# Chunk 4's projections and chunk 1's output projection as row pairs, in other stages

## The chip, the cores and the metric

The kernel runs on one core of one Trainium2 chip. The metric is the device time of one launch in microseconds (us), the median of several runs. TensorE is called PE, VectorE DVE, ScalarE ACT, GpSimd POOL and SyncE SP, as in the profile.

## The reference

One block of a transformer over 2048 rows of 576 columns, in bf16. `c` gives six rows of modulation. Attention is local: each row looks at 8 rows, itself and every second row before it; there are 32 heads of 18 columns.

```python
mod = (_silu(c) @ w_mod).reshape(c.shape[0], 6, 1, -1)
sa, ca, ga, sb, cb, gb = ...
h = _layernorm(x) * (1 + ca) + sa
x = x + ga * _A_ref(h, A_wqkv, A_wo)         # local attention, W = 8, dil = 2
h = _layernorm(x) * (1 + cb) + sb
x = x + gb * _B_ref(h, B_w_gate, B_w_up, B_w_down)   # ((h @ w_gate) * (h @ w_up)) @ w_down
```

The wide layer has 4608 columns, so nearly all of PE's work is gate, up and down.

## The kernel before

**Tiles and stages.** The rows are 8 chunks of 256 (`CH`), each of 2 tiles of 128 rows (`ST`). Chunks go through the wide layer in the groups `[[0], [1, 2], [3, 4], [5, 6], [7]]` (`GROUPS`). A setup does chunk 0's attention and part of the next chunks'. Then each group has a *gate/up* stage (36 column tiles `f`, `gate_up`) and a *down* stage (36 row tiles `f`, `down`). Projections, attention and norms of later chunks are put between the matmuls of these stages. The first gate/up takes chunk 0 (256 columns for each matmul) and has beside it chunk 3's Q, K and V, chunk 1's attention, and the start of chunk 2's. The first down has, before the change, chunk 4's Q, K and V, chunk 1's output projection and second norm, and chunk 2's values and output projection.

**Two forms of matmul.** 576 is four and a half times 128. In the plain form (`a_q`, `a_v`, `b_w`) a product takes five matmuls of 128 rows, and the rows 64 to 127 of the fifth (`KF`) hold zeros. In the paired form (class `Pair`: gate/up, `qk_pair`, `v_pair`, `w_pair`) two products run at once in the upper and the lower 64 rows, nine steps each, and swap halves between `first` and `second`. Then the fifth row tile must hold the same 64 rows twice: `both_halves` and `wo_both` copy these rows in the weights (on POOL, L1325 and L871), and the norm writes the last 64 columns a second time (argument `both`, L298 and L307), so that the transposed tile has them in both halves. A pair's matmuls are queued so that the next pair's `first` goes ahead of this pair's `second`. A pair holds two of PSUM's eight banks (`psp`); they are freed when ACT has cast them (L821, L822: `u_sb`, `g_sb`) or DVE has read them.

**The order.** Every engine runs its instructions in the order of the program. `timed` plans it: `items` are the stage's own column tiles with their PE time, `extra` are the pairs to be put between them, and `threads` are lists of pieces `(PE time, DVE time, what it needs, its mark, wait until the mark holds, call)`. The planner counts a time `t` for PE and one for DVE, and issues a piece when its need is marked by then and DVE isn't too far behind. What is left when a gate/up stage ends (`late`) goes into the following down. `gbg` holds the lists of each gate/up, `first_down` and `next_down` those of the downs.

**Chunk 1's second norm.** `b_w(1, j)` multiplies `oT` by `wo` and DVE adds the result to the row (L659 to L663); `b_ln(1)` takes the statistics on DVE; `b_norm(1)` normalizes on ACT (L290 to L308); `b_td(1)` transposes with two DMAs from SP's queue into `h2T` (L689), and `b_mod(1)` modulates that tile, its column blocks 3 and 4 on ACT (L325), 0 to 2 on DVE (L323). The second gate/up begins with chunk 1's half of it. `b_o(2)` is the transpose of chunk 2's attention on PE, with two copies to `oT` on ACT (L577, L578); `b_w(2, j)` uses `oT`. `a_t4` transposes chunk 4's normalized rows on PE.

**DMA queues.** SP issues the gate/up weights (L158), rows (L140, L144) and transposes. POOL issues the down weights (`load_wd`, L175), the write of V to DRAM (`vd`) and its reading with the eight offsets (`b_ld`, L481, 1152 KB). `behind` makes a DMA wait for another's landing. Blocks of down weights that have no buffer of their own are put in memory that is free for a while: blocks 5 and 6 of the first group in `prod_t` (`ld_prods(0)`), once the products of chunk 2 have been used.

Of the kernel before, what the change touches and what calls it, by code (L numbers as in the profile page):

```python
# [22 lines left out]
KF = 4  # L23
# [16 lines left out]
GC = D // 4  # L40

GROUPS = [[0], [1, 2], [3, 4], [5, 6], [7]]
PAIRED = (3, 5, 7)


@with_exitstack
def kernel(
# [13 lines left out]
    nc = tc.nc  # L61
# [259 lines left out]
    def modulate(dst, s, m, vi_scale, vi_shift, on_dve):  # L321
        if on_dve:
            nc.vector.tensor_scalar(dst, s, modc[:, vi_scale, m:m + 1], modc[:, vi_shift, m:m + 1], ALU.mult, ALU.add)  # L323
        else:
            nc.scalar.activation(dst, s, ACTF.Identity, bias=modc[:, vi_shift, m:m + 1], scale=modc[:, vi_scale, m:m + 1])  # L325

    def transposed(src, dst, cols, vi):
        n = P * len(cols)
        pA = ps([P, 3, n], BF, "tr_pA")
        pB = ps([P, 2, n], BF, "tr_pB")  # L330
        for m in range(KT):
            d = pA[:, m, :] if m < 3 else pB[:, m - 3, :]
            for c, j in enumerate(cols):
                nc.tensor.transpose(d[:, js(c)], src[:, j, m * P:(m + 1) * P], ident[:])

        def evict(first_on_dve=True):
            for m in range(KT):
                s = pA[:, m, :] if m < 3 else pB[:, m - 3, :]
                modulate(dst(m), s, m, vi + 1, vi, (m < 3) == first_on_dve)
        return evict  # L340

    def mod_columns(wm, pi, fill=lambda: None, steps={}, order=(KF, 0, 1, 2, 3)):
# [49 lines left out]

    def a_ln(i):
        x = x_in.pop(i)
        xn, rsq, norm = layernorm(lambda j: x[:, j, :], "a", i in (3, 4), i in (3, 5, 6, 7))
        aa[i] = dict(xn=xn, rsq=rsq, norm=norm)

    def a_norm(i):
# [21 lines left out]
            nc.sync.dma_start_transpose(out=aa[i]["hT"][:, :, js(j)], in_=aa[i]["xn"][:, j, :])  # L420

    def a_t4():
        a_t(4, False)
        nc.gpsimd.memset(aa[4]["hT"][64:, KF, :], 0.0)

    def a_mod(i, ms, on_dve=True):
        hT = aa[i]["hT"]
# [47 lines left out]
    def b_ld(i, j):  # L475
        b = bb.setdefault(i, dict(prod={}, vsh={}))
        base = HALO + i * CH + j * P - DIL * (W - 1)
        vsh = vshp.tile([P, W, DH, H], BF, name="vsh")
        vsrc = bass.AP(vd.tensor, vd.offset + base * D, [[D, P], [DIL * D, W], [1, D]])
        b["vsh"][j] = vsh  # L480
        return nc.gpsimd.dma_start(vsh[:].rearrange("p w d h -> p w (d h)"), vsrc)  # L481

    def b_p(i, w):
        b = bb.setdefault(i, dict(prod={}, vsh={}))
# [240 lines left out]
    def values_of(i, nxt=None):  # L725
        r = []
        for j in range(ST):
            r += [(0, 0.75, f"a{i}", "-", 0, lambda j=j, w=w: b_mul(i, j, w)) for w in range(0, W, 2)]
            r += [(0, 0.75, "", "-", 0, lambda j=j: b_add(i, j, 0)), (0, 0.75, "", "-", 0, lambda j=j: b_add(i, j, 1)),
                  (0, 1.2, "", f"o{i}{j}", 0, lambda j=j: b_add(i, j, 2))]  # L730
            if i in PAIRED:
                r.append((0, 0, "", f"O{i}" if j == ST - 1 else "-", 11.0 if i == 7 else 14.0, lambda j=j: b_od(i, (j,))))
            if nxt is not None:

                r.append((0, 0, f"v{nxt}", "-", 0, lambda j=j: behind(b_ld(nxt, j), bb[i]["od"]) if (i, j) == (3, 1) else b_ld(nxt, j)))
        return r
# [153 lines left out]

    QKP = [(0, 1), (2, 3), (4,), (5, 6), (7, 8)]

    def timed(items, extra, threads, slack, busy=0.0):

        t, dve = 0.0, busy
        done, seq = {f"v{i}": 0.0 for g in GROUPS for i in g[1:]}, []
        done["late"] = 0.0
        extra, threads = list(extra), [list(th) for th in threads]

        def ready(need):  # L900
            return all(done.get(x, 1e9) <= t for x in need.split())

        def fill():
            nonlocal t, dve
            moved = True
            while moved:
                moved = False
                for th in threads:
                    if th and ready(th[0][2]) and (not th[0][1] or dve <= t + slack):
                        pe, d, _, mark, wait, call = th.pop(0)  # L910
                        t += pe
                        dve = max(dve, t) + d if d else dve
                        done[mark] = (dve if d else t) + wait
                        seq.append(("piece", call))
                        moved = True
                        break
        for kind, f, step, own, need in items:
            if seq and extra and ready(extra[0][1]):
                pe, _, mark, make, *ve = extra.pop(0)
                seq.append(("pair", make))  # L920
                t += pe
                dve = max(dve, t) + sum(ve)
                done[mark] = t + pe + 1.0
                fill()
            assert ready(need), (need, t)
            seq.append((kind, f))
            fill()
            dve = max(dve, t) + own
            t += step
        assert not extra, (extra[0][1], t)  # L930
        return seq, [(*p[0:2], p[2] if all(x in names(th) for x in p[2].split()) else "late", *p[3:]) for th in threads for p in th]

    def names(th):
        return [p[3] for p in th]
# [397 lines left out]
    def ld_prods(gi):  # L1332
        for k in range(2):
            g = gi * NBLK + (5 if gi == 0 else 3) + k
            wd_home[g] = prod_t[:, k * FB * D:(k + 1) * FB * D].rearrange("p (k d) -> p k d", d=D)
            r = load_wd(g)
            if gi:
                behind(r, wgu_in[gi * NBLK + NBLK - 1])

    loads = {(0, 23): lambda: behind(load_wd(1), bb[2]["ltd"]), (0, 24): lambda: ld_d1(4), (0, 25): lambda: load_wd(2), **{(gi, 32): lambda gi=gi: ld_prods(gi) for gi in (1, 2, 3)}, (3, 34): wgu_spaces, (NG - 1, 28): lambda: [ld_spare(k) for k in range(4)]}  # L1340

# [5 lines left out]
    def gb_row():  # L1347
        gb_cols(lambda k: wm5()[:, k, :] if k < KF else wm5r[:])
        ld_d1(3)

    first = attention_of(1, 2)[12:-14]
    first = [(0, 0, "", "p17", 2.2, nop), (0.75, 0, "p17", "l14", 1.0, lambda: b_l(1, 4)), (0.35, 0, "l14", "t14", 0.3, lambda: b_lt(1))] + first

    first[1:8] = [first[1], first[3], first[4], first[2], first[7], first[5], first[6]]
# [2 lines left out]
    at = [k for k, p in enumerate(first) if p[2] == "v2"][0]  # L1357
    first.insert(at + 4, (0, 0, "v2", "-", 0, lambda: behind(b_ld(2, 0), wgu_in[8])))
    first.pop(at)
    at = [k for k, p in enumerate(first) if p[3] == "o11"][0] + 2  # L1360
    first.insert(at, (0, 0, "o11", "O1", 0, nop))
    gbg = {0: (qkv_of(3, "p17 z3"),
               [[(0, 0, "", "-", 0, lambda: (load_wm5(), load_wd(0))), (0, 0, "", "z3", 8.0, both_halves), (0, 0, "", "w5", 12.0, nop), (0.85, 0, "w5", "-", 0, gb_row), (0, 0, "", "-", 0, lambda: load_res(2))],
                norm_of(3, "", "", 5) + [(0, 2.5, "", "m4", 0.2, lambda: a_ln(4)), (0, 0, "m4", "r4", 1.0, lambda: aa[4]["rsq"]()),
                                         (0, 0, "r4", "e4", 2.0, lambda: aa[4]["norm"]((0,))), (0, 0, "e4", "n4", 1.6, lambda: aa[4]["norm"]((1,))),
                                         (0, 0, "n4 v3", "x4", 0, nop)],
               first, [(0, 0, "y1", "s1", 0.6, lambda: b_exp(1))]]),
           1: (qkv_of(5, "p37") + wo_of(3),
               [[(0, 0, "", "-", 0, lambda: (loads_v(3), load_res(3), load_res(4), wo_both()))], norm_of(5, "p33", "", 7), second]),
           2: (qkv_of(6, "") + wo_of(5),  # L1370
               [[(0, 0, "", "h6", 1.0, lambda: (loads_v(5), load_res(5), load_res(6)))], attention_of(5, 6)]),
           3: (qkv_of(7, "") + wo_of(7), [[(0, 0, "", "h7", 1.0, lambda: load_res(7)), (0, 0, "v7", "-", 0, lambda: loads_v(7))], [(0, 0, "q74", "-", 0, nop)] + prods_of(7) + softmax_of(7) + values_of(7)]),
           4: ([], [])}

    def first_down(late):
        def q(g):
            return (0.53 if g == 2 else 1.07, 0, "h4", "-", 0, lambda: a_q(4, g))

        def v(j):
            return (1.2, 0, "h4", "-", 0, lambda: a_v(4, j))  # L1380

        def out_1(first):
            return [(0, 0, "", "o0", 0.4, nop), (0.55, 0, "o0", "o1", 1.9, lambda: b_o(1)), (1.2, 1.35, "o1", "-", 0, lambda: b_w(1, 0)), (1.2, 1.35, "", "x1", 0.5, lambda: b_w(1, 1)),
                    (0, 2.5, "", "s1", 0.7, lambda: b_ln(1)), (0, 0, "s1", "n1", 2.3, lambda: b_norm(1)), (0, 0, "n1", "t1", 9.5, lambda: b_td(1)),
                    (0, 1.0, "t1", "-", 0, lambda: (b_mod(1, (3, 4), False), b_mod(1, (0, 1, 2), True)))]
        assert not {"O1", "x4"} & set(names(late))
        a4 = [(0.6, 0, "", "h4", 1.7, lambda: (a_t4(), load_x(6), ld_prods(0)))]
        o2 = [(0, 0, "o21", "z2", 0.6, nop), (0.55, 0, "z2", "O2", 1.1, lambda: b_o(2)), (1.2, 1.35, "O2", "-", 0, lambda: b_w(2, 0)), (1.2, 1.35, "", "x2", 0.2, lambda: b_w(2, 1)),
              (0, 2.2, "", "s2", 0.7, lambda: b_ln(2)), (0, 1.5, "s2", "n2", 0.2, lambda: b_norm(2)), (0.55, 1.0, "n2", "-", 0, lambda: b_t(2))]
        return [a4, out_1(True), late + [(0, 0, "", "a2", 0.0, nop)] + values_of(2) + o2, [q(0), q(1), q(2), q(3), q(4), v(0), v(1)]]  # L1390

    def norm2_of(i, need):
        return [(0, 2.3, need, f"s{i}", 0.7, lambda: b_ln(i)), (0, 1.5, f"s{i}", f"n{i}", 0.2, lambda: b_norm(i)),
# [12 lines left out]
    left = []  # L1406
    for gi, grp in enumerate(GROUPS):
# [13 lines left out]
        if gi == NG - 1:  # L1421
            down_last(gi, hh)
        else:
            left = down(gi, hh, first_down(late) if gi == 0 else next_down(gi, late))
            assert gi == 0 or not left


# [28 lines left out]
```

## Time and profile before

| what | us |
|---|---|
| median of 3 runs | 540.21 (540.2 to 541.58) |
| the profiled execution | 540.27 |
| its span | 538.0 |
| first gate/up, in the trace | 48.1 to 94.0 |
| first down | 94.0 to 125.7 |
| second gate/up, begins | 125.7 |
| PE busy | 531.7 |
| DVE, ACT, POOL busy | 318.4, 253.0, 73.1 |

Windows of the trace over these stages give the share of the other engines: in the first gate/up (45.9 us) DVE is busy 37.1 us and ACT 35.4, in the first down (31.7 us) DVE 22.4 and ACT 14.1. Busy time of PE is from the start of a matmul to its modelled end, so that a matmul's duration (0.27 us for 256 columns) is longer than the step from one to the next; steps are read from the starts. A wait is the idle time of an engine in front of an instruction and is put down to what came last.

### The profile page before, as it was taken

To read this page: it belongs to the slowest core of one execution; us is meant where nothing else is said; L and a number is where in the kernel's file an instruction comes from. 1 tells how busy PE (TensorE), PEld (TensorE's weight loads), DVE (VectorE), ACT (ScalarE), POOL (GpSimd) and SP (SyncE) were. 2 spreads that over 40 slices of the span, in tenths; PEclk is the share of its full clock that TensorE was granted. 3 is DMA by queue.
4 is the path that set the end of the run, shared out by engine and by line. 5 is a ranking of instruction groups with operands and counts; after the bars stand their busy time and mean duration, and the time that the engine had idled before them with its cause. 6 is when DMAs were issued, how large, how long until landed. Compare 5 with 4: busy or idle time off the path is not lost.

```text
span 538.0 us, 14722 instructions
## 1 busy us (share of the span) xinstructions
PE 531.7 (99%) x6244; PEld 321.2 (60%) x6244; DVE 318.4 (59%) x731; ACT 253.0 (47%) x620; POOL 73.1 (14%) x113
## 2 busy tenths in 40 slices
PE   8999999999999999999999999999999999999997
PEld 4787888657745454555544454555544454558875
DVE  5899787858766788527467797514527733032212
ACT  4866877634656553013555543104556542006630
POOL 8105013212000110111000010110010101110210
PEclk9999999999999999999999999999999999999999
DMA  9999999889853862999345964973395694759731
GB/s 288 286 290 366 311 266 339 299 138 351 282 145 92 269 198 45 247 291 310 104 156 130 232 211 128 224 233 111 102 306 160 158 302 81 233 139 297 254 96 41
DMA packets 94659, 114.47 MB, mean 213 GB/s; under 512 B 27873, under 2 KB 83378, under 8 KB 94466
## 3 DMA queue, kind: packets, MB, share of 16 engines
q1 hardware_dynamic: 82864, 66.92, 45.5%
q0 software_dynamic: 11424, 46.40, 28.3%
q8 instruction: 49, 0.80, 0.7%
q10 hardware_dynamic: 306, 0.21, 0.1%
q14 instruction: 16, 0.13, 0.1%
HBM read 103.07 MB, written 4.74 MB: 200 GB/s over the span
## 4 chain that ended last, share of the span: by engine, by line
PE 96%; DVE 2%; DMA 1%; SPq 0%; issue 0%; ACT 0%
PE pg L770 28%; PE pu L770 23%; PE acc L1007 20%; PE pq L442 4%; PE pq L770 3%; PE accr L1012 3%; PE acc L1062 3%; PE pv L770 2%; PE pw L659 2%; PE pv L465 2%; PE lgT L499 1%; DMA wmA<-in_w_mod_dram 1%; PE pw L770 1%; PE po L614 1%; DVE prod_t L487 1%; PE pwj L636 0%
## 5 line engine op out<-in xcount | busy, mean ns | idle before, releaser
L770 PE MATMUL pg<-h2T,wgu 64*128 64x512 bf16 (+1 forms) x1376 | 266.4, 331 | 0.0
L770 PE MATMUL pu<-h2T,wgu 64*128 64x512 bf16 (+1 forms) x1376 | 265.5, 331 | 0.0
L770 PEld LDWEIGHTS <-wgu 64*128 64x128 bf16 x2752 | 133.9, 94 | 94.8
L821 ACT CAST u_sb<-pu 128x512 bf16<-128x512 f32 (+1 forms) x172 | 85.6, 498 | 150.5 <-PE pg L770 150.0
L824 DVE TENSOR_TENSOR hh<-g_sb,u_sb 128x512 bf16<-128x512 bf16 x136 | 58.3, 429 | 115.0 <-ACT g_sb L822 114.0
L822 ACT CAST g_sb<-pg 128x512 bf16<-128x512 f32 (+1 forms) x172 | 86.7, 504 | 0.0
L1007 PE MATMUL acc<-wd,hh 128*128 128x512 bf16 x344 | 86.1, 380 | 0.0
L1007 PEld LDWEIGHTS <-hh 128*128 128x128 bf16 x504 | 49.0, 98 | 59.2 <-issue 1.5
L1012 PE MATMUL accr<-wd,hh 128*128 128x64 bf16 x344 | 62.4, 193 | 0.0
L770 PE MATMUL pu<-h2T,wgr 64*128 64x512 bf16 (+1 forms) x188 | 61.4, 327 | 0.5 <-DVE dd L528 0.5
L770 PE MATMUL pg<-h2T,wgr 64*128 64x512 bf16 (+1 forms) x188 | 61.4, 327 | 0.0
L1012 PEld LDWEIGHTS <-hh 128*128 128x128 bf16 x504 | 45.8, 98 | 1.2
L175 POOL DMA_DIRECT2D wd<-in_B_w_down_dram x29 | 21.9, 754 | 173.7 <-PE accr L1012 138.1
L548 DVE TENSOR_TENSOR vsh<-vsh,attn 128x1152 bf16<-128x1152 bf16 x56 | 39.8, 752 | 0.0
L487 DVE TENSOR_TENSOR prod_t<-qT,kT 128x1280 bf16<-128x1280 bf16 x36 | 28.3, 820 | 3.3 <-ACT kT L841 2.7
L1007 PE MATMUL acc<-prod_t,hh 128*128 128x512 bf16 x112 | 28.2, 380 | 0.0
L770 PEld LDWEIGHTS <-wgr 64*128 64x128 bf16 x376 | 18.5, 94 | 15.8 <-issue 2.8
L481 POOL DMA_DIRECT2D vsh<-vd x14 | 12.6, 899 | 95.7 <-DVE o_sb L556 76.1
L325 ACT ACTIVATE h2T<-h2T,modc 128x256 bf16<-128x256 bf16 x12 | 6.6, 593 | 33.6 <-DMA h2T<-xn 33.6
L442 PE MATMUL pq<-hT,wqk 128*128 128x256 bf16 (+1 forms) x225 | 21.7, 251 | 0.1
L770 PE MATMUL pq<-hT,wqk 64*128 64x256 bf16 (+1 forms) x360 | 21.6, 258 | 0.0
L1012 PE MATMUL accr<-prod_t,hh 128*128 128x64 bf16 x112 | 21.6, 193 | 0.0
(225 smaller groups left out, 627.7 us busy)
## 6 DMA issues: line engine op xcount, KB each, us to landing
wgu<-in_B_w_gate_dram SPq DMA_DIRECT2D x41, 512.0 KB, 5.0
wgu<-in_B_w_up_dram SPq DMA_DIRECT2D x41, 512.0 KB, 6.8
wd<-in_B_w_down_dram POOLq DMA_DIRECT2D x29, 576.0 KB, 5.8
vsh<-vd POOLq DMA_DIRECT2D x14, 1152.0 KB, 9.3
prod_t<-in_B_w_down_dram POOLq DMA_DIRECT2D x8, 576.0 KB, 6.3
hh<-in_B_w_down_dram POOLq DMA_DIRECT2D x6, 576.0 KB, 7.1
x_t<-in_A_x_dram SPq DMA_DIRECT2D x8, 288.0 KB, 5.8
x_r<-in_A_x_dram SPq DMA_DIRECT2D x8, 288.0 KB, 8.2
```

What stands on the lines that cost most here:

```text
L175: return nc.gpsimd.dma_start(wb[:], B_w_down[r0:r0 + FB * P, :].rearrange("(k p) n -> p k n", p=P))
L442: nc.tensor.matmul(pq[:, gi, :], lhsT=wqk[:, kt, m * P:(m + 1) * P], rhs=hT[:, kt, cols], start=(kt == order[0] and not (by_k and gi)), st ...
L481: return nc.gpsimd.dma_start(vsh[:].rearrange("p w d h -> p w (d h)"), vsrc)
L487: nc.vector.tensor_tensor(prod, aa[i]["qT"][:], aa[i]["kT"][:, :, off:off + CH], ALU.mult)
L548: nc.vector.tensor_tensor(v, v, at, ALU.mult)
L770: return nc.tensor.matmul(out, lhsT=lhs, rhs=rhs, start=first, stop=last, skip_group_check=True)
L821: nc.scalar.copy(u[:, c, :], pu)
L822: nc.scalar.copy(g[:, c, :], pg)
L824: return lambda: nc.vector.tensor_tensor(hh[:, f - c:f + 1, :], g, u, ALU.mult)
L1007: nc.tensor.matmul(acc[j][:], lhsT=hh[:, f, js(j)], rhs=wb[:, f % FB, 0:512], start=(f == 0), stop=(f == FT - 1))
L1012: nc.tensor.matmul(accr[:, j, :], lhsT=hh[:, f, js(j)], rhs=wb[:, f % FB, 512:D], start=(f == 0 and j == 0), stop=(f == FT - 1), skip_grou ...
L1062: nc.tensor.matmul(acc[i][:], lhsT=hh[:, f, js(j)], rhs=wb(f)[:, c0:c1], start=(f == 0), stop=(f == FT - 1))
```

## The change

- Chunk 4's Q and K become five pairs, chunk 1's output projection two pairs; all seven are put in the first gate/up, most of them behind its last column tiles (`timed` now issues pairs left over when the items are through). Chunk 4's V becomes two pairs early in the second gate/up. With that, chunk 1 counts as `PAIRED` (its `o_sb` gets its last 64 columns twice, by `o_tail`; chunk 2's tail is set to zero), and chunk 4's norm writes `both`.
- `a_t4` and `b_o(1)` become one piece of the first gate/up. All five modulations of `a_t4` run on DVE (before: two on DVE, three on ACT), and the memset on POOL goes.
- Chunk 1's `b_ln` goes into the first gate/up; `b_norm`, `b_td` and `b_mod` come at the start of the first down. Chunk 2's first value products get the earliest times 52.5 and 56.5 (`V2`, `W2`).
- `both_halves` and `wo_both` are issued behind `gb_row` (before: at the start of the first gate/up, and of the second).
- `ld_prods(0)` stays in the first down, but its two loads wait for the landing of `b_ld(2, 0)`.

```diff
-PAIRED = (3, 5, 7)
+PAIRED = (1, 3, 5, 7)
...
         def evict(first_on_dve=True):
             for m in range(KT):
                 s = pA[:, m, :] if m < 3 else pB[:, m - 3, :]
-                modulate(dst(m), s, m, vi + 1, vi, (m < 3) == first_on_dve)
+                modulate(dst(m), s, m, vi + 1, vi, first_on_dve == 5 or (m < 3) == first_on_dve)
...
-        xn, rsq, norm = layernorm(lambda j: x[:, j, :], "a", i in (3, 4), i in (3, 5, 6, 7))
+        xn, rsq, norm = layernorm(lambda j: x[:, j, :], "a", i in (3, 4), i >= 3)
...
     def a_t4():
-        a_t(4, False)
-        nc.gpsimd.memset(aa[4]["hT"][64:, KF, :], 0.0)
+        a_t(4, 5)
+        load_x(6)
...
-        return nc.gpsimd.dma_start(vsh[:].rearrange("p w d h -> p w (d h)"), vsrc)
+        r = nc.gpsimd.dma_start(vsh[:].rearrange("p w d h -> p w (d h)"), vsrc)
+        b.setdefault("ld", r)
+        return r
...
-            if i in PAIRED:
+            if i in PAIRED[1:]:
...
+        for x in extra:
+            done.pop(x[2], None)
...
-        assert not extra, (extra[0][1], t)
-        return seq, [(*p[0:2], p[2] if all(x in names(th) for x in p[2].split()) else "late", *p[3:]) for th in threads for p in th]
+        for pe, need, mark, make, *_ in extra:
+            assert ready(need), (need, t)
+            seq.append(("pair", make))
+            t += pe
+            done[mark] = t + pe + 1.0
+            fill()
+        parts[:] = [[(*p[0:2], p[2] if all(x in names(th) for x in p[2].split()) else "late", *p[3:]) for p in th] for th in threads]
+        return seq, [p for th in parts for p in th]
...
-            if gi:
-                behind(r, wgu_in[gi * NBLK + NBLK - 1])
+            behind(r, wgu_in[gi * NBLK + NBLK - 1] if gi else bb[2]["ld"])
...
-    first = attention_of(1, 2)[12:-14]
+    first = attention_of(1, 2)[12:]
+    first.insert(-14, (0, 0, "V2", "-", 0, nop))
+    first.insert(-7, (0, 0, "W2", "-", 0, nop))
...
-    gbg = {0: (qkv_of(3, "p17 z3"),
-               [[(0, 0, "", "-", 0, lambda: (load_wm5(), load_wd(0))), (0, 0, "", "z3", 8.0, both_halves), (0, 0, "", "w5", 12.0, nop), (0.85, 0, "w5", "-", 0, gb_row), (0, 0, "", "-", 0, lambda: load_res(2))],
+    gbg = {0: (qkv_of(3, "p17 z3") + wo_of(1) + qkv_of(4, "p27")[:5],
+               [[(0, 0, "", "-", 0, lambda: (load_wm5(), load_wd(0))), (0, 0, "", "z3", 8.0, nop), (0, 0, "", "w5", 12.0, nop), (0.85, 0, "w5", "-", 0, gb_row), (0, 0, "", "-", 0, lambda: (load_res(2), both_halves(), wo_both()))],
...
+               [(0, 2.5, "W11", "S1", 0.7, lambda: b_ln(1)), (0, 0, "S1", "N1", 2.3, lambda: b_norm(1)), (0, 0, "N1", "T1", 9.5, lambda: b_td(1)),
+                       (0, 1.0, "T1", "-", 0, lambda: (b_mod(1, (3, 4), False), b_mod(1, (0, 1, 2), True)))],
+               first, [(1.15, 0, "o11 n4 v3", "O1", 2.3, lambda: (a_t4(), b_o(1))), (0, 0, "O1", "h4", 0.6, nop)],
+               [(0, 0, "y1", "s1", 0.6, lambda: b_exp(1))], [(0, 0, "", "V2", 52.5, nop)], [(0, 0, "", "W2", 56.5, nop)]]),
+           1: (qkv_of(4, "")[5:] + qkv_of(5, "p37") + wo_of(3),
+               [[(0, 0, "", "h4", 0, lambda: (loads_v(3), load_res(3), load_res(4)))], norm_of(5, "p33", "v4", 7), second]),
...
-    def first_down(late):
-        def q(g):
-            return (0.53 if g == 2 else 1.07, 0, "h4", "-", 0, lambda: a_q(4, g))
...
+    def first_down(parts):
         o2 = [(0, 0, "o21", "z2", 0.6, nop), (0.55, 0, "z2", "O2", 1.1, lambda: b_o(2)), (1.2, 1.35, "O2", "-", 0, lambda: b_w(2, 0)), (1.2, 1.35, "", "x2", 0.2, lambda: b_w(2, 1)),
               (0, 2.2, "", "s2", 0.7, lambda: b_ln(2)), (0, 1.5, "s2", "n2", 0.2, lambda: b_norm(2)), (0.55, 1.0, "n2", "-", 0, lambda: b_t(2))]
-        return [a4, out_1(True), late + [(0, 0, "", "a2", 0.0, nop)] + values_of(2) + o2, [q(0), q(1), q(2), q(3), q(4), v(0), v(1)]]
+        return [[(0, 0, "", "-", 0, lambda: ld_prods(0))]] + parts[:-1] + [parts[-1] + o2]
...
-            left = down(gi, hh, first_down(late) if gi == 0 else next_down(gi, late))
+            left = down(gi, hh, first_down([th for k, th in enumerate(parts) if th and k != 3] + [parts[3]]) if gi == 0 else next_down(gi, late))
```

More of the change, by code (lines that the diff above doesn't have):

```diff
@@ L891 @@
     QKP = [(0, 1), (2, 3), (4,), (5, 6), (7, 8)]
+    parts = []
     def timed(items, extra, threads, slack, busy=0.0):
@@ L1359 @@
     first.pop(at)
-    at = [k for k, p in enumerate(first) if p[3] == "o11"][0] + 2
-    first.insert(at, (0, 0, "o11", "O1", 0, nop))
-    gbg = {0: (qkv_of(3, "p17 z3"),
-               [[(0, 0, "", "-", 0, lambda: (load_wm5(), load_wd(0))), (0, 0, "", "z3", 8.0, both_halves), (0, 0, "", "w5", 12.0, nop), (0.85, 0, "w5", "-", 0, gb_row), (0, 0, "", "-", 0, lambda: load_res(2))],
+    gbg = {0: (qkv_of(3, "p17 z3") + wo_of(1) + qkv_of(4, "p27")[:5],
+               [[(0, 0, "", "-", 0, lambda: (load_wm5(), load_wd(0))), (0, 0, "", "z3", 8.0, nop), (0, 0, "", "w5", 12.0, nop), (0.85, 0, "w5", "-", 0, gb_row), (0, 0, "", "-", 0, lambda: (load_res(2), both_halves(), wo_both()))],
                 norm_of(3, "", "", 5) + [(0, 2.5, "", "m4", 0.2, lambda: a_ln(4)), (0, 0, "m4", "r4", 1.0, lambda: aa[4]["rsq"]()),
[L1365 to L1369, printed above, removed]
+                                         (0, 0, "r4", "e4", 2.0, lambda: aa[4]["norm"]((0,))), (0, 0, "e4", "n4", 1.6, lambda: aa[4]["norm"]((1,)))],
+               [(0, 2.5, "W11", "S1", 0.7, lambda: b_ln(1)), (0, 0, "S1", "N1", 2.3, lambda: b_norm(1)), (0, 0, "N1", "T1", 9.5, lambda: b_td(1)),
[4 more added lines that the diff above has]
+               [[(0, 0, "", "h4", 0, lambda: (loads_v(3), load_res(3), load_res(4)))], norm_of(5, "p33", "v4", 7), second]),
            2: (qkv_of(6, "") + wo_of(5),
@@ L1373 @@
            4: ([], [])}
-    def first_down(late):
-        def q(g):
-            return (0.53 if g == 2 else 1.07, 0, "h4", "-", 0, lambda: a_q(4, g))
[L1379 to L1387, printed above, removed]
+    def first_down(parts):
         o2 = [(0, 0, "o21", "z2", 0.6, nop), (0.55, 0, "z2", "O2", 1.1, lambda: b_o(2)), (1.2, 1.35, "O2", "-", 0, lambda: b_w(2, 0)), (1.2, 1.35, "", "x2", 0.2, lambda: b_w(2, 1)),
               (0, 2.2, "", "s2", 0.7, lambda: b_ln(2)), (0, 1.5, "s2", "n2", 0.2, lambda: b_norm(2)), (0.55, 1.0, "n2", "-", 0, lambda: b_t(2))]
-        return [a4, out_1(True), late + [(0, 0, "", "a2", 0.0, nop)] + values_of(2) + o2, [q(0), q(1), q(2), q(3), q(4), v(0), v(1)]]
+        return [[(0, 0, "", "-", 0, lambda: ld_prods(0))]] + parts[:-1] + [parts[-1] + o2]
     def norm2_of(i, need):
```

## The prediction

> **What bounds the kernel now.** I read the page first, then the waits of PE, then the timelines of PE, DVE, POOL, SP and ACT around the first gate/up (48.1 to 94.0 us in the trace) and the first down (94.0 to 125.7).
>
> ```profile
> PE 531.7 (99%) x6244; PEld 321.2 (60%) x6244; DVE 318.4 (59%) x731; ACT 253.0 (47%) x620; POOL 73.1 (14%) x113
> ```
>
> PE is busy 99% of the span at a granted clock of 1.0, so only two things change the time: fewer columns through PE, and more or fewer waits of PE. The waits view has one that concerns the changed stages:
>
> ```profile
> PE pu L770 <- DVE dd L528: 0.5, 1, 0.5
> ```
>
> DVE's timeline shows where this comes from:
>
> ```profile
> 51.58 1.07 DVE L824 TENSOR_TENSOR hh<-g_sb,u_sb 128x512 bf16<-128x512 bf16 x1 [0.33 <-issue]
> ...
> 54.89 0.42 DVE L824 TENSOR_TENSOR hh<-g_sb,u_sb 128x512 bf16<-128x512 bf16 x1
> ...
> 57.75 0.69 DVE L528 TENSOR_TENSOR dd<-lg,mx 128x512 f32<-128x512 bf16 x1
> ```
>
> The same product takes 1.07 us once and 0.42 us elsewhere. After it DVE runs without a pause up to `dd`, whose end frees the bank that PE waits for. Beside the long product POOL makes its row copies:
>
> ```profile
> 52.47 1.19 POOL L1325 COPY wqk<-wqk 64x1152 bf16<-64x1152 bf16 x1
> 53.60 0.66 POOL L1325 COPY wv<-wv 64x576 bf16<-64x576 bf16 x1
> ```
>
> The work that the change repacks lies in the first down, on PE alone:
>
> ```profile
> 97.14 1.26 PE L442 MATMUL pq<-hT,wqk 128*128 128x256 bf16 x10
> 98.23 0.47 PE L657 MATMUL pwr<-wo,oT 128*128 128x64 bf16 x5
> 98.54 1.24 PE L659 MATMUL pw<-wo,oT 128*128 128x512 bf16 x5
> 99.62 1.26 PE L442 MATMUL pq<-hT,wqk 128*128 128x256 bf16 x10
> 100.71 0.31 PE L657 MATMUL pwr<-wo,oT 128*128 128x64 bf16 x5
> 100.86 1.24 PE L659 MATMUL pw<-wo,oT 128*128 128x512 bf16 x5
> 101.94 2.89 PE L442 MATMUL pq<-hT,wqk 128*128 128x256 bf16 x25
> 104.67 1.23 PE L465 MATMUL pv<-wv,hT 128*128 128x504 bf16 x5
> ```
>
> Last, the transposes of chunk 1's normalized rows (`b_td(1)`), from SP's timeline, the h2T tile's view and ACT's timeline:
>
> ```profile
> 109.92 2.62 SPq L689 DMA_TRANSPOSE h2T<-xn  x2
> ```
>
> ```profile
> DMA to landing us min/median/max: 7.2/9.1/11.1
> ```
>
> ```profile
> 117.08 1.01 ACT L577 COPY oT<-oT_pA 128x1024 bf16<-128x1024 bf16 x1 [6.09 <-PE oT_pA L576]
> ...
> 122.39 1.10 ACT L325 ACTIVATE h2T<-h2T,modc 128x256 bf16<-128x256 bf16 x2 [4.02 <-DMA h2T<-xn]
> ```
>
> The second transpose, issued at 111.23, lands 11.1 us later. ACT waits for it 4.0 us, and nobody else does: chunk 2's copies to `oT` (117.08) came before that wait in ACT's order. This order is what the change turns round.
>
> **The change part by part.** The profiled run took 540.27 us (span 538.0 and 2.27 around it), 0.06 over the median of 540.21. The sum is made against 540.27.
>
> *Matmuls.* From start to start, chunk 4's Q and K take 1.09 + 1.09 + 2.73 = 4.91 us, chunk 1's projection 1.39 + 1.23 = 2.62, chunk 4's V 2.44 (104.67 to 107.11): 9.97. As pairs, two 64-row halves start every 0.109 us at 256 columns (gate/up halves at 85.82, 85.93, 86.04), so a pair is 9 × 0.109 = 0.98: four pairs 3.92, the half-width pair 0.49. At 288 columns the chain has 1.10 for 18 halves: two V pairs and two projection pairs 4.40. Sum 8.81, saved 1.16. Chunk 4's and chunk 1's transposes only move.
>
> *One more change of shape.* That piece (`a_t4`, `b_o(1)`) now stands between gate/up pairs. Around the transposes at 130.5, which stand so now, PE loses 0.15 us before and 0.10 behind. Cost 0.25.
>
> *Row copies later.* They move behind `gb_row` on POOL, which is held there for `gd` (issued 63.40, landed 69.19) and issues two more loads until 70.83; with the `wo` copy (0.68 at 128.78 now) they end near 73.4. The hh product at 51.58 loses its 0.64 excess, so `dd` ends some 0.5 earlier and PE's wait of 0.48 goes: -0.48 (bounds -0.6 and 0). In the new place DVE modulates chunk 3's hT (70.63 to 71.99), which QK3's first pair needs at 73.12. That is 1.1 us of cover against a stretch of 0.64: taken at nothing; `wqk`'s copy ends at 72.0, 1.1 before its use. The Trainium skill ("SBUF — State Buffer", 🔬 SBUF: two separate sides) says that the port pair which DVE and GpSimd share is a lock, and the loser stands for the whole instruction. By that rule both copies (1.19 + 0.66) could hold DVE 1.85 us, QK3 would be 0.7 late, and the sum 0.7 higher. The trace agrees that an instruction is stretched beside a copy, but by 0.64 (51.58) and 0.44 (128.75, 0.87 against 0.43), less than a copy.
>
> *Banks.* PSUM has 8, a pair holds 2. The new piece takes four at once for transposes, between f=32 and f=33. They start near 90.1; `tr_pB` is free only after the five modulates, now all on DVE, which stand behind `b_sm0(2)` (in the trace 1.7 us up to 91.5, here 91.1): 5 × 0.32 gives 92.8. PE, with f=33's first and f=32's second half done, asks again at 92.4. Cost 0.5; bounds 0 and 1.1 (ACT must also do `b_exp(2)`, both `oT` copies, 1.01 + 0.38, and f=32's casts, to 93.5). The row nearest is the wait above, one bank held for 2.7 us.
>
> *ACT in the first gate/up.* xn of chunk 4 gets its second half too, two 64-column activations of 0.43. ACT runs without a gap from 75.8 to 82.3 and PE loses nothing; two 0.35 steps more are taken at nothing, 0.3 if the cover is short. `o_tail` adds 0.18 twice and 0.09 twice on DVE, idle 0.5 to 1.5 there between products.
>
> *Two down blocks.* Without the memset that held POOL to 97.1, blocks 5 and 6 wait for `b_ld(2,0)` (landed 96.32) and are asked at about 96.4 instead of 97.6. The shorter down reads them from f=20, near 112: covered by 8 us.
>
> *First down.* It would begin at S = 94.05 + 8.0 (the moved transposes 1.1, 0.25, pairs 2.2 + 4.4) - 0.48 + 0.5, about 102.0. Following `timed` through the new lists, `b_td(1)` comes early, then after f=24 first `b_mod(1)`, then `b_o(2)`, and after f=27 `b_w(2,0)`. PE reaches `b_w(2,0)` at S + 0.15 + 28 × 0.49 + 0.53 = S + 14.4. DVE, in order, ends `b_ln(1)` near S + 0.6, ACT ends QK4's last copies at S + 0.9, and from the first activation of the norm to the second transpose's issue it is 3.5 us (107.74 to 111.23): issue at S + 4.4. POOL asks for block 7 behind f=3 (S + 2.1), block 8 behind f=7 (S + 4.1) and block 9 behind f=11 (S + 6.1). In the trace the second transpose of a pair with a POOL load issued within half a microsecond of it took 11.1 us (111.23) and 11.8 (216.91, a load 0.2 before, chunk values 0.5 behind); with the load 1.0 us later or more, 4.8 (335.02) and 5.3 (452.20). Block 8 falls within half a microsecond, so I take 11.1, also the row of the same transfer. Then it lands at S + 15.5, ACT's two modulates (1.10) and `oT` copy (1.01) follow, and `oT` is there at S + 17.7. Who is queued behind ACT's wait: `b_o(2)`'s copies, and behind these PE at `b_w(2,0)`, which stands 17.7 - 14.4 = 3.3 us. With 4.8 us to landing it waits nothing, with 11.8 4.0. Nothing hides it, because the remaining down matmuls are behind it on PE.
>
> *Second gate/up.* Two V pairs among the first `f0` bring `b_t(2)` to PE some 3.8 us into the stage instead of 4.8 (125.7 to 130.5). Chunk 2's norm is ready 4.2 in (130.4 now, less 0.44 for the copy that is gone): cost 0.35, bounds 0 and 0.7.
>
> Sum: -1.16 + 0.25 - 0.48 + 0.5 + 3.3 + 0.35 = +2.8, so **543.0**.
>
> **The rivals.** *A: the transposes land in time.* At up to 7.7 us to landing `b_w(2,0)` finds its `oT`; what remains is -0.5, 539.7. For it: 4.8 and 5.3 above, and DMA has less to move near S than it had at 94. Against: three blocks are asked 2 us apart, where the old schedule had two. *B: in between,* 8 to 9.6 us: 539.9 to 541.5. *C: every new wait is hidden.* Then -1.16 - 0.48 = -1.6, plus 0.25 if the shape change costs: 538.6 to 538.9. This is the case on the other side: the point where it decides is a second transpose under 7.7 us together with DVE freeing the transposes' banks before 92.4. *D: the page's lock.* DVE's modulation of chunk 3 is held by both copies, QK3 waits 0.7: 543.7 with the forecast, 540.4 with A. I put it at 1 in 10 within each case.
>
> **How the numbers follow.** About 0.3% (1.6 us) can be told from no change. Forecast 0.50 (slower by more than that in nearly all of it), A 0.20, B 0.15, C 0.15. In C half falls beyond 1.6 us, and A reaches there when its bank wait is nothing too; I give 0.15 to faster. Slower is 0.50, same 0.35. The range reaches down to C's 538.7, and up to 544.4, the forecast with 11.8 to landing and the upper bank bound. The forecast's own range is 541.9 to 544.4.
>
> **What would show it.** Right: among the waits of PE, `pwr` L657 behind ACT's `oT`, some 3 us near 116, with ACT's L325 on h2T ahead of the `oT` copy and waiting for the transposes' landing; hh near 51.6 at 0.42; PE's wait for `dd` gone; a short wait of a gate/up pair near 92.4 for a transposes' bank. Wrong: ACT's modulates of h2T start before about 114, or `oT` is copied before them; then the time is 539 to 540. If PE waits at QK3 near 73, the copies' new place is the cause.

## The result, and the profile after

| | us |
|---|---|
| kernel before, median of 13 runs | 540.20 (539.48 to 541.86) |
| changed kernel, median of 13 runs | 541.87 (540.88 to 544.67) |
| ratio | 1.003, 95% interval 1.0017 to 1.0042 |
| changed kernel, its profiled execution | 544.67, span 542.7 |

The change makes the kernel slower by 0.3%, 1.67 us. The profiled execution is the slowest of the thirteen: it has two losses of its own, which are named below and which a second profile of the same kernel (542.07) does not have.

The shares of the engines are as before, PE a point lower:

```profile
PE 532.6 (98%) x6293; PEld 325.6 (60%) x6321; DVE 320.2 (59%) x740; ACT 252.1 (46%) x625; POOL 72.5 (13%) x112
```

The waits of PE (in total, times, longest). The wait for `dd` (0.5 before) is gone, and three others stand in the changed stages:

```profile
PE pwr L659 <- ACT oT L579: 2.0, 1, 2.0
...
PE pq L772 <- DVE hT L323: 0.3, 1, 0.3
PE pq L772 <- ACT qT L841: 0.3, 1, 0.3
```

The timelines of DVE and POOL show both sides of the moved row copies. First the hh product at the front, 1.07 us before and 0.43 now:

```profile
50.94 0.43 DVE L826 TENSOR_TENSOR hh<-g_sb,u_sb 128x512 bf16<-128x512 bf16 x1 [0.33 <-issue]
```

Then the copies' new place, with DVE's modulation of chunk 3's hT beside them. Those five instructions took 1.37 us before and now take 3.92 (the first row is the kernel before, the others the changed kernel):

```profile
70.63 1.37 DVE L323 TENSOR_SCALAR hT<-hT,modc 128x256 bf16<-128x256 bf16 x5
```

```profile
70.40 1.17 POOL L1337 COPY wqk<-wqk 64x1152 bf16<-64x1152 bf16 x1
71.48 0.69 POOL L1337 COPY wv<-wv 64x576 bf16<-64x576 bf16 x1
72.09 0.68 POOL L873 COPY wo<-wo 64x576 bf16<-64x576 bf16 x1
```

```profile
69.96 3.92 DVE L323 TENSOR_SCALAR hT<-hT,modc 128x256 bf16<-128x256 bf16 x5
```

Taken one by one, the first of the five lasts 2.90 us alone, to 72.86, which is 0.09 behind the end of the third copy (72.77). The added 2.55 us are the length of all three copies (1.17 + 0.69 + 0.68).

In the first down, ACT's timeline shows the order that the prediction rests on: first the wait for the transposes, then chunk 1's modulation, then chunk 2's `oT` (before, `oT` came first). The h2T tile's view has the transposes:

```profile
117.93 1.09 ACT L325 ACTIVATE h2T<-h2T,modc 128x256 bf16<-128x256 bf16 x2 [10.42 <-DMA h2T<-xn]
118.93 0.99 ACT L579 COPY oT<-oT_pA 128x1024 bf16<-128x1024 bf16 x1
119.82 0.37 ACT L580 COPY oT<-oT_pB 128x256 bf16<-128x256 bf16 x1
```

```profile
DMA to landing us min/median/max: 6.4/8.2/10.1
```

PE stands from 117.77 to 119.97 (from the start of the last matmul to the start of the next). Windows of the trace behind it show what this profile alone has (the columns: busy time of PE, PEld, DVE, ACT and POOL with counts, granted clock, DMA share, GB/s):

```profile
120.50:121.00 0.50, 0.50 (x4) 0.26 (x3) 0.21 (x1) 0.00 (x0) 0.00 (x0) 1.00 1.09 348
121.00:121.50 0.50, 0.50 (x3) 0.18 (x2) 0.00 (x0) 0.00 (x0) 0.00 (x0) 0.59 1.09 348
...
124.00:124.50 0.50, 0.50 (x3) 0.15 (x1) 0.22 (x1) 0.00 (x0) 0.00 (x0) 0.50 0.43 143
```

From 121.1 to 124.5 the clock is granted at half, which costs 1.7 us. The other loss is a single pause of 0.5 us at 68.1, for which the profile names nothing ("issue"). In the second profile the wait for `oT` is 1.6, and the second transpose lands after 9.6 us.

For the comparisons I use two readings of the traces. One is the length of the three changed stages, from the first matmul of one to the first of the next. The other is PE's loss in a stretch: the steps between starts of its matmuls, less the nominal step of their shape (0.107 us for a half of 256 columns; undisturbed steps are 0.109, so that a stretch without a wait still shows 0.1 to 0.4, and the first stretch of the table, with more shapes in it, 1.04; what counts there is the difference). Stretches count from the start of the first gate/up; QK3 and QK4 are the pairs for Q and K of chunks 3 and 4. All later stages are equal to 0.01 us in all kernels, but for the end of the last one, which is 0.17 us shorter in the two kernels with DMAs. The second gate/up of the kernel before begins at 125.90, 0.2 later than the table ahead of the prediction has it; the kernel before has this one trace.

| trace | first gate/up | first down | second gate/up | sum | loss 6 to 20 (`dd`) | 24 to 27.5 (QK3) | 27.5 to 34 (ACT) |
|---|---|---|---|---|---|---|---|
| before | 45.92 | 31.86 | 82.45 | 160.23 | 1.49 | 0.14 | 0.16 |
| changed, first profile | 56.02 | 24.76 | 84.76 | 165.54 | 1.04 | 1.08 | 0.98 |
| changed, second profile (e8_after_again) | 54.92 | 22.64 | 84.76 | 162.32 | 1.04 | 0.45 | 1.01 |
| e1_order | 55.28 | 20.76 | 84.76 | 160.80 | 1.04 | 0.80 | 1.01 |
| e2_copies_back | 54.15 | 22.51 | 84.76 | 161.42 | 1.47 | 0.08 | 0.21 |
| e10_both_again | 54.34 | 20.76 | 84.76 | 159.86 | 1.46 | 0.09 | 0.21 |
| e9_idle_again | 53.78 | 20.76 | 84.76 | 159.30 | 1.04 | 0.08 | 0.26 |

### The profile page after: what moved, and what is told of

Same layout as the page of the kernel before. It is cut to its first block, busy times and chain, and to the rows that moved or that the text cites. A ratio compares the mean times of both kernels' runs of the same rounds, so it can differ in the third digit from the quotient of the medians.

```text
span 542.7 us, 14854 instructions
## 1 busy us (share of the span) xinstructions
PE 532.6 (98%) x6293; PEld 325.6 (60%) x6321; DVE 320.2 (59%) x740; ACT 252.1 (46%) x625; POOL 72.5 (13%) x112
## 4 chain that ended last, share of the span: by engine, by line
PE 92%; DMA 2%; DVE 2%; ACT 2%; issue 1%; SPq 0%; DVEq 0%; ACTq 0%
PE pg L772 28%; PE pu L772 23%; PE acc L1019 17%; PE pq L772 3%; PE accr L1024 3%; PE pq L442 3%; PE acc L1074 3%; PE pv L772 2%; DMA h2T<-xn 2%; PE pw L772 2%; PE lgT L501 1%; PE pw L661 1%; PE pv L465 1%; PE po L616 1%; DVE hT L323 1%
## 5 line engine op out<-in xcount | busy, mean ns | idle before, releaser
L772 PEld LDWEIGHTS <-wgu 64*128 64x128 bf16 x2752 | 136.7, 94 | 94.0 <-issue 0.7
L1019 PE MATMUL acc<-wd,hh 128*128 128x512 bf16 x328 | 84.7, 383 | 0.1
L772 PE MATMUL pq<-hT,wqk 64*128 64x256 bf16 (+1 forms) x450 | 28.0, 259 | 0.6 <-DVE hT L323 0.3
L772 PEld LDWEIGHTS <-wqk 64*128 64x128 bf16 x450 | 21.7, 94 | 7.2 <-issue 1.3
L1047 DVE TENSOR_TENSOR t_r<-accr,gb_bc 128x256 bf16<-128x256 f32 (+1 forms) x4 | 1.5, 378 | 39.7 <-PE accr L1024 39.7
```

The source lines that it names most:

```text
L772: return nc.tensor.matmul(out, lhsT=lhs, rhs=rhs, start=first, stop=last, skip_group_check=True)
L1019: nc.tensor.matmul(acc[j][:], lhsT=hh[:, f, js(j)], rhs=wb[:, f % FB, 0:512], start=(f == 0), stop=(f == FT - 1))
```

## The experiments

The kernels ran in three groups, each beside its own runs of the kernel before. The runs of one kernel lie 2 to 6 us apart. Part of this arises before the changed stages: the first gate/up begins between 47.5 and 49.7 us in the traces. So the verdicts on single waits rest on the traces, and the times say whether the sum agrees. In the first group (the four kernels with 541.16 beside them) it doesn't quite: by the traces these four are 0.6 to 1.4 us slower than the trace of the kernel before, an execution of 540.27, but none is clear of the kernel before beside it. Set against the changed kernel's ratios (1.003 and 1.0023), those of e1, e2 and e6 fit their sums; e5's does not.

| kernel | median | before, beside it | ratio, 95% interval |
|---|---|---|---|
| e1_order | 540.97 | 541.16 | 0.9998 (0.9983 to 1.0013) |
| e2_copies_back | 541.03 | 541.16 | 1.0004 (0.9988 to 1.002) |
| e5_before_dma | 540.65 | 541.16 | 0.9996 (0.998 to 1.0013) |
| e6_blocks | 540.72 | 541.16 | 0.9993 (0.9976 to 1.0009) |
| e3_both | 539.79 | 540.53 | 0.9979 (0.9963 to 0.9995) |
| e7_idle | 539.63 | 540.53 | 0.9976 (0.9961 to 0.9992) |
| e4_dma | 540.31 | 540.53 | 0.999 (0.9966 to 1.0014) |
| e8_after_again | 542.62 | 540.53 | 1.0023 (1.0003 to 1.0042) |
| e9_idle_again | 540.00 | 540.36 | 0.9989 (0.9979 to 0.9998) |
| e10_both_again | 539.97 | 540.36 | 0.9994 (0.998 to 1.0009) |

**Is it the order on ACT?** e1_order keeps the change and lets chunk 1's modulation come one place later, behind `b_o(2)`:

```diff
-(0, 0, "N1", "T1", 9.5, lambda: b_td(1))
+(0, 0, "N1", "T1", 9.6, lambda: b_td(1))
```

> The changed kernel with one number altered: T1's delay in the planner 9.5 -> 9.6, so that b_o(2) with its copies to oT is issued ahead of b_mod(1). Theory O (order on ACT): PE's wait at b_w(2,0) for oT (2.0 us in the trace of the changed kernel) goes, and the slow clock behind it with it; 541.9 - 2.2 = 539.7 or a little less, ratio to before 0.998 to 0.999; the transposes land as late as they did. Rival M (the wait moves): the transposes' landing holds someone else instead, DVE's reading of b_w(2,0)'s banks or the second gate/up's first matmuls; then PE waits 1 to 2 us there and the ratio stays near 1.003.

The wait for `oT` is gone and the first down is 20.76 us, while the second transpose still takes 9.41 us to land. So the slow transpose costs nothing by itself: it costs what stands behind it on ACT. The clock stays whole, and rival M, a wait that moves elsewhere, falls. The time is 541.0 and not the 539.7 expected. The other loss of the changed kernel stays, in another dress: the hh product ahead of the hT pieces is now the one that stands beside the copies (2.33 us; POOL's first copy is at 70.75).

```profile
70.47 2.33 DVE L826 TENSOR_TENSOR hh<-g_sb,u_sb 128x512 bf16<-128x512 bf16 x1 [0.80 <-ACT g_sb L824]
```

**Is it the loads beside the transposes?** e6_blocks leaves ACT's order as the change has it, but blocks 8 and 9 of the down weights wait for the second transpose's landing:

```diff
+            tds[i] = nc.sync.dma_start_transpose(...)
...
+                    r = load_wd(gi * NBLK + k)
+                    if gi == 0 and k in (8, 9):
+                        behind(r, tds[1])
```

> The changed kernel, with the loads of down blocks 8 and 9 made to wait for the landing of chunk 1's second transpose. Theory Q (POOL's loads in flight slow the transposes): the second transpose lands 4 to 6 us after its issue instead of 10.1, ACT's modulates start near 113 and PE doesn't wait for oT: 541.9 - 2.2 = 539.7, ratio 0.999. Rival (the transposes are slow by themselves or by SP's own loads behind them): 9 to 11 us again, the 2 us wait stays, ratio 1.003 or more since the blocks come later.

The view of the h2T tile and ACT's timeline:

```profile
DMA to landing us min/median/max: 4.1/4.4/4.7
```

```profile
112.05 1.09 ACT L325 ACTIVATE h2T<-h2T,modc 128x256 bf16<-128x256 bf16 x2 [4.46 <-DMA h2T<-xn]
```

The second transpose lands after 4.14 us in place of the changed kernel's 10.1 and 9.6, and there is no wait for `oT`. SP's weight loads were asked 1.3 us behind it as before; so it is the two loads that POOL asks for 0.1 and 2.1 us behind it, together, that make it slow; which of them weighs more was not tried. Order and loads are two independent ways to the same 20.76.

**Is it the copies' place?** e2_copies_back puts them at the start of the stage again; the first down stays as the change has it:

```diff
-"z3", 8.0, nop)
+"z3", 8.0, lambda: (both_halves(), wo_both()))
...
-lambda: (load_res(2), both_halves(), wo_both())
+lambda: load_res(2)
```

> The changed kernel with the three row copies on POOL back at the start of the first gate/up. Theory L (lock): the five modulates of chunk 3's hT take 1.4 us again instead of 3.9, QK3's first pair doesn't wait (some 1.3 us at 72 to 74 us), ACT's bunching at 79 (0.4) goes too; the first hh product is long again and PE's wait for dd is 0.5 longer. Sum -1.2: 540.7, ratio 1.001; the wait for oT stays. Rival (QK3's pair is late for its own reason, the weights' copies or hT's transposes): the wait at 72 stays and the time is 541.9 or more.

The five hT pieces take 1.42 again, and PE's waits are these:

```profile
PE pwr L659 <- ACT oT L579: 1.4, 1, 1.4
...
PE pu L772 <- DVE dd L530: 0.5, 1, 0.5
```

With the copies away, both waits near QK3 go, the one behind hT and also the one behind ACT's qT: PE's loss is 0.08 in the first stretch (0.45 to 1.08 in the kernels with all three copies late) and 0.21 in the second (about 1.0). So ACT's backlog is no cost of the added columns of chunk 4's norm: it follows from DVE's delay. The first gate/up is 0.77 us shorter than in the second profile of the changed kernel: moving the copies won 0.43 (`dd`) and lost 1.2.

**Are the copies what stretches DVE, or the loads that POOL issues ahead of them?** e5_before_dma is the kernel before, with the copies as DMAs of SP:

```diff
-nc.gpsimd.tensor_copy(w_t[64:, KF, 0:n], w_t[0:64, KF, 0:n])
+nc.sync.dma_start(w_t[64:, KF, 0:n], w_t[0:64, KF, 0:n])
```

> The kernel before with the row copies made by DMAs from SP's queue instead of instructions on POOL, at the same places. Theory L: the first hh product takes 0.42 us instead of 1.07, PE's wait for dd falls from 0.5 to some 0.1 us, and chunk 2's norm is not stretched in the second gate/up: 540.2 - 0.5 = 539.7, ratio 0.999. Rival (POOL's DMA issues, not its copies, stretch the product): the product stays at 1.07 us and the ratio at 1.000.

The product is at 0.43 with POOL's loads still beside it, so the copies stretch it. In this profile the gain did not arrive: the first gate/up is 46.80, longer by 0.9, and the first down 32.42, longer by 0.6, with these two waits, one in each:

```profile
PE pv L770 <- ACT kT L841: 0.9, 1, 0.9
...
PE pw L659 <- DVE x L661: 0.4, 1, 0.4
```

**What is left of the pairs when both losses are undone?** e3_both has e1's and e2's edits together, e4_dma also the copies as DMAs of SP, and e7_idle has e1's edit, with the copies of `wqk` and `wv` held until a product that ends near 60, ahead of a gap of DVE, and `wo`'s copy where the change has it:

```diff
-            nc.gpsimd.tensor_copy(w_t[64:, KF, 0:n], w_t[0:64, KF, 0:n])
+            behind(nc.gpsimd.tensor_copy(w_t[64:, KF, 0:n], w_t[0:64, KF, 0:n]), bb[2]["lastp"])
...
+(0, 0, "w5", "-", 0, both_halves), (0.85, 0, "w5", "-", 0, gb_row),
```

> The changed kernel with both single undoings at once: row copies at the start of the first gate/up again, and chunk 1's residual rows one place later, so that ScalarE empties chunk 2's transposed attention rows first. Theory T (the two losses are separate and what is left is the pairs alone): first gate/up as with the copies alone, 54.15 us, first down as with the order alone, 20.76, second gate/up 84.76, together 159.67, that is 0.56 under the kernel before (160.23); ratio 0.999. In the waits no oT, no qT and no hT; the wait for dd of 0.5 is back. Rival U (the wait of the first down comes from what the earlier stage leaves in the queues, so that it moves with the copies): a wait for oT of 1 to 1.6 us is back, the three stages give 161 to 161.4, ratio 1.001.

> As with the order alone (residual rows later), but POOL's copies of the rows of wqk and wv wait for a product of chunk 2's logits that ends near 60, in front of a gap of VectorE of 1.5 us; the copy of wo's rows stays where the change put it. Theory L (a copy costs only what VectorE does beside it): the first hh product keeps 0.43 and the wait for dd stays under 0.3 as in the changed kernel, and the five hT pieces take 1.4 to 1.7 as in the kernel before, with no wait for qT near 79: first gate/up 53.6 to 53.8 us, first down 20.76, second gate/up 84.76, together 159.0 to 159.3, 0.9 to 1.2 under the kernel before; ratio 0.998. Rival B (the backlog of ScalarE near 79 belongs to chunk 4's two norms of 64 columns or to the pairs, not to the copies): 0.45 stays there, first gate/up 54.1. Rival P (a copy that waits for VectorE slips, and its shares of the port fall on the next hh product and the sums of chunk 1): the product near 62.3 takes 1 us or more and the wait moves to a matmul near 66, first gate/up 54.2 or more.

> As with both undoings, and the three row copies are DMAs of SP in place of copies of POOL. Theory L: nothing stretches VectorE's hh product (0.43) nor its five hT pieces, and the wait for dd is gone: first gate/up 53.6 to 53.8, sum of the three stages 159.0 to 159.3. Rival G (what is won at the front is given back, as it was in the kernel before with DMAs: ScalarE's copies then fall together and a matmul waits 0.9 for kT near 82 and 0.4 for a residual near 102): first gate/up 54.2 to 54.9, sum 159.7 to 160.4, no gain over the copies at the start.

e3_both's time came out 0.74 under the kernel before. Its first down is 20.76 without a wait for `oT`, so rival U falls. But its profile fell on its slowest execution (542.74; the sum is 162.84), and shows how much the copies cost when they fall badly. DVE's and POOL's timelines:

```profile
51.74 2.55 DVE L826 TENSOR_TENSOR hh<-g_sb,u_sb 128x512 bf16<-128x512 bf16 x1 [0.33 <-issue]
```

```profile
52.24 1.17 POOL L1337 COPY wqk<-wqk 64x1152 bf16<-64x1152 bf16 x1
53.32 0.68 POOL L1337 COPY wv<-wv 64x576 bf16<-64x576 bf16 x1
```

The same product took 1.05 in e2_copies_back, where POOL's copy began 0.86 us behind its start; here it began 0.50 behind. The traces with the copies in a row all follow this: where the first copy's record begins 0.85 to 0.89 behind the start of the DVE instruction, that instruction is 0.6 longer (before, e2, e10); where it begins at most 0.50 behind, the instruction lasts until 0.3 behind the second copy (e1, e3, e6, e8) or 0.1 behind the third (the first profile). The chain up to `dd` is 1.5 us later, PE stands 2.2 us, and then the clock is at half (windows of this trace):

```profile
60.00:60.50 0.50, 0.37 (x4) 0.29 (x6) 0.50 (x2) 0.00 (x0) 0.00 (x0) 0.63 1.07 346
60.50:61.00 0.50, 0.50 (x10) 0.35 (x6) 0.50 (x2) 0.00 (x0) 0.00 (x0) 0.50 1.10 348
...
63.50:64.00 0.50, 0.50 (x14) 0.43 (x10) 0.00 (x0) 0.50 (x2) 0.00 (x0) 0.96 1.11 349
```

e7_idle and e4_dma kept the product at 0.42 and 0.43 and had no waits for `dd`, hT or qT, so that rival B falls; the product beside e7's copy of `wv` took 0.62, less than rival P's 1 us. But PE lost 0.83 and 1.08 in front of chunk 3's first V pair; the first gate/up was 55.21 and 55.39 in place of the 53.6 to 53.8 expected, so that nothing of the gain at the front was left, as rival G has it for e4_dma (it had 54.2 to 54.9). The profile names ACT's kT:

```profile
PE pv L772 <- ACT kT L843: 0.6, 1, 0.6
```

The program has that pair wait for the two kT copies that end at 82.74 in e7_idle; PE starts at 83.65, and for the weight load just ahead of it the profile names nothing (0.90 us idle, "issue"). What ended 0.26 to 0.32 us ahead of it in all three traces with this wait (e4, e5, e7) is the landing of a gate block of weights: asked near 71.8, landed at 83.24 to 83.43, where in traces without the wait (before, after, e1, e2, e6, e8) it landed at 77.9 to 79.8.

**Does that wait belong to the kernel?** The two best kernels ran once more, and the changed kernel as well:

> The kernel with the copies in VectorE's gap, once more. In its first profile the gate half of a weight block asked at 71.9 landed at 83.4, four to five us later than in the profiles without a wait there, and TensorE stood 0.83 in front of chunk 3's first V pair until 83.65. Theory D (the transfers of the front are full, and how late a block lands differs from one execution to the next): where that block lands before 80 there is no wait in front of V, first gate/up 53.8 to 54.4 us, the first hh product again 0.43; where it lands after 83, the wait is back and the stage is 55.0 to 55.3. Rival K (the wait belongs to the program: V waits for ScalarE's copy of kT): 0.8 to 0.9 again, with the block before 80 too. Time 0.5 to 1.3 under the kernel before.

> The kernel with the copies at the start and the residual rows later, once more. In its first profile, one of the slowest of its executions, the hh product beside the copies took 2.55 us, the matmul behind dd waited 2.0 and the clock fell to half for 3.6 us. Theory T: in a profile where that product takes 1.0 to 1.1 the wait for dd is 0.5 and the clock stays whole: first gate/up 54.1 us, first down 20.76, second gate/up 84.76, sum 159.6, 0.6 under the kernel before. Rival V (with the residual rows later the product always starts inside the copies): 2.5 us and a wait of 2.0 again, with the half clock behind it, first gate/up 57.3. Time 0.4 to 1.0 under the kernel before.

> The changed kernel once more, beside the others. Theory W (the wait for oT is what makes it slower; the stretch at half clock in its first profile was one of a kind): a wait for oT of 1.5 to 2.5 us, the second transpose 9.5 to 10.5 us from issue to landing, no stretch at half clock; first gate/up 55.3 to 55.6, first down 22.5 to 23.1, together 162.5 to 163.5; time 1.2 to 2.0 us over the kernel before, ratio 1.002 to 1.004. Rival H (the clock always falls behind that wait): granted 0.5 for about 3 us right behind the wait again, first down 24.5 or more. Rival N (the whole difference was scatter of the first chip): ratio 0.999 to 1.001.

In e9_idle_again the same program has no wait in front of V, and the block landed at 80.9, between the two cases of the expectation; the first gate/up is 53.78 and the sum 159.30, 0.93 under the kernel before. Rival K falls. (That this execution took 540.76 all the same, the slowest of its twelve, comes from what is ahead of these stages: its first gate/up begins at 49.67. The median is 0.36 under the kernel before, less than the 0.5 to 1.3 expected.) That the late landing is the cause is not shown: PE's pair does not read that block, and what it stood for stays open. POOL's and DVE's timelines, the copies in the gap:

```profile
61.82 1.14 POOL L1337 COPY wqk<-wqk 64x1152 bf16<-64x1152 bf16 x1 [8.66 <-DMA hh<-in_B_w_up_dram]
62.91 0.66 POOL L1337 COPY wv<-wv 64x576 bf16<-64x576 bf16 x1
```

```profile
72.10 1.72 DVE L323 TENSOR_SCALAR hT<-hT,modc 128x256 bf16<-128x256 bf16 x5
```

Against e1_order, PE, DVE, ACT and SP have the same instructions in the same order; only two copies of POOL stand elsewhere, and the first gate/up is 1.5 us shorter. Against e8_after_again it is 1.14 shorter. That is what the change's place for the copies costs. In e10_both_again the product took 1.05, the wait for `dd` 0.4, and the clock stayed whole: sum 159.86, 0.37 under the kernel before (0.6 was expected), so rival V falls. e8_after_again repeats the changed kernel's result in another group of runs (1.0023) with a wait for `oT` of 1.6 and no half clock: rivals H and N fall.

e7_idle's kernel is faster than the kernel before in both of its groups (0.9976 and 0.9989, neither interval reaching 1), by 0.1 to 0.24%, and faster than the changed kernel where that ran beside it (539.63 against 542.62). That is less than this study's bound of 0.3%, but its stages show where it comes from.

## Why the prediction was right, and where it was wrong

The forecast was 543.0, slower, because the first down waits for `oT`. Measured were 541.87, slower, and that wait is the largest term. The size is at the lower edge of the forecast's own range (541.9 to 544.4; its terms give 544.3 at the upper end), and it is that near partly by luck, because errors cancel. Its terms, against the traces (the second profile of the changed kernel, where nothing else is said; its sum is 162.32 - 160.23 = +2.1, forecast +2.8):

| term | forecast | measured | from |
|---|---|---|---|
| pairs, shape, banks, `b_t(2)` together | -0.06 | -0.56 | 54.15 + 20.76 + 84.76, against 160.23 |
| row copies, gain at the front | -0.48 | -0.43 to -0.45 | loss 6 to 20: 1.49 to 1.04 |
| row copies, new place | 0 | +1.2 (1.5 in e1) | 54.92 - 54.15 + 0.43; e1 - e9 |
| PE at `b_w(2,0)` for `oT` | +3.3 | +1.9 | 22.64 - 20.76 |

- *The wait for `oT`*: right in mechanism, place and size class. With S the start of the first down, PE reached `b_w(2,0)` at S + 14.3 (forecast S + 14.4), and the second transpose was issued at S + 4.25 (S + 4.4). It landed after 10.1 us in the first profile and 9.6 in the second, in place of 11.1, and the wait was 2.0 and 1.6 in place of 3.3. The mis-sized step is the time to landing, taken from the same transfer in the kernel before; 8.1 to 10.3 is what nine traces with both loads show in the new place. Its two conditions, the order on ACT and the loads beside, were each shown by undoing one (e1, e6).
- *The row copies' gain*: right.
- *Their new place, "taken at nothing"*: wrong. This is the step that failed. I had a row for a stretch of 0.64 and took it as the price of any meeting with a copy, under 1.1 us of cover. In the first profile the five hT pieces took 2.55 us longer (3.92 against 1.37), in the second the product ahead of them took 1.98 us and they 1.71; QK3 was late, and ACT's later copies met QK4's pairs, which is another 0.8. The Trainium skill ("SBUF — State Buffer", 🔬 SBUF: two separate sides) says that the port pair of DVE and GpSimd is a lock and the loser stands for the whole instruction. The trace of before spoke against the whole price, and the traces of after agree with the page that the loser stands, and go beyond it: one instruction stood through two copies in a row, or through three. Rival D, at 1 in 10, came true beside the forecast.
- *ACT's backlog*: I priced it at 0, or 0.3 with short cover, as a cost of the added columns. It cost 0.8 in the changed kernel and nothing in e2, e9 and e10, which have the same columns.
- *Banks, +0.5*: oversized. From its own times (92.8 less 92.4) it is 0.4. The five modulates end at 94.3, and PE lost about 0.1 there in the first profile (a step of 0.195 in place of 0.109); the short wait for a bank that the prediction names as a sign is not in the waits. *`b_t(2)`, +0.35*: about 0.1. *Pairs*: -1.16 + 0.25 = -0.91 against -0.56 with both small waits in it, so about -0.8.

The errors cancel in part: 1.4 too much for `oT`, 0.5 too much for the small waits, 1.2 too little for the copies' new place. Of the rivals, A's condition (a transpose in under 7.7 us) was met only where e6 made it, and C needed it too. B's (8 to 9.6 us) is where the second profile lies, with 9.6 us at its upper edge, so forecast and B are not far apart here.

## What to carry to other kernels

A copy on POOL has no fixed price: the same DVE product took 0.43 us without copies beside it, and 1.05 or 2.55 beside the same copies, by half a microsecond of phase. So cost the meeting at the full length of all copies in a row, and look for a gap of DVE for them before looking for a later place. Not every DVE instruction pays: in the kernel before, the statistics (L283) beside the copies took 0.44 to 0.45 us each, as without copies. When a wait for a DMA is moved on an engine, read what stands behind it on that engine: the transpose of 10 us was free as soon as the 1.4 us of copies that PE needs stood ahead of it. And before crediting a change with removing a wait at the front, see what the same stretch waits for next, in more than one profile.

## What was not expected of the hardware

- A pause of PE of 2.2 us, counted from start to start, was followed by a granted clock of half for 3.4 us, both times that one occurred (at 117.8 in the changed kernel, at 57.9 in e3_both), at a cost of some 1.7 us: in e3_both the halves of 256 columns then start every 0.207 us in place of 0.109. After pauses of 1.62 (e2_copies_back) and 1.75 (e8_after_again) it stayed whole. The Trainium skill ("TensorE: Matmul & The Clock Gate", What's actually happening) gives half speed after an idle window of about 3.4 us, counted on a free-running clock; the length of the slow stretch (3.41 us) agrees with that window, but the pause that came before it was shorter.
- A DMA transpose of the same tile took 4.1 us where POOL's next two loads were held back (one trace) and 8.1 to 10.3 where they were asked 0.1 and 2.1 us behind it (nine traces), with SP's loads asked at the same time.
- A weight block of the front landed between 77.9 and 83.4 for requests at 70.9 to 72.7, in kernels with nearly the same program, so that one profile of that stage says little about waits near 83.
